# Loading q token-major behind the keys and transposing it with the DMA crossbar, in an attention and feed-forward kernel

## The chip, the cores and the metric

One Trainium2 chip, one core. The metric is the device time of one execution in microseconds (us). Profiles are single executions; the first instruction of the profile is time zero in every "at" below. The span in a profile is 1.7 to 1.8 us shorter than the time of the same execution. The granted clock is the share of TensorE's full clock that the chip allowed it, as the profile records it.

## The reference

Four batches of sparse-sorted attention feed a feed-forward layer with a squared ReLU. The feed-forward products dominate; the attention of later tiles is woven between them.

```python
B, H, S, D = 4, 8, 768, 64; n_blocks = 8          # block = 96 rows
# P: sort_net after five rounds of exp and row/column normalisation
k_sorted = einsum('bhij,bhjcd->bhicd', P, k_blocks)
v_sorted = einsum('bhij,bhjcd->bhicd', P, v_blocks)
scores   = scale * q_block @ k_sorted_block.T      # per block of 96 rows
out      = softmax(scores) @ v_sorted_block
x = out.transpose(0, 2, 1, 3).reshape(3072, 512)
g = s * relu(x @ w_in)**2 + b                      # w_in 512 x 2048
result = g @ w_out                                 # w_out 2048 x 512, float32 out
```

## The kernel before: what the change and the argument touch

A batch is two tiles of 384 tokens. QT[b] is q of a batch turned so that the head dimension lies on the partitions; the scores need it. In the kernel before, q of batch 1 comes in rows of 768 B and TensorE turns it; q of batches 2 and 3 already comes token-major (rows of 128 B) and is turned by DMA transposes (transfers that transpose on their way, through the DMA crossbar) that SP issues. Token-major means that each row of 128 B is one token of one head. Transfers issued by GpSimd are in the software queue (q0 in the profile), those of SP in the hardware queue (q1). Values of batch 1 are sorted on TensorE, stored to DRAM (`dv`) and read back in another layout (`vs`), also by SP. A GpSimd sum over w_out (`csum`) goes through one product (`bias_piece`) that stands ahead of the scores in TensorE's order.

```python
def load_q(b, part=slice(0, 128)):                 # GpSimd issues: the software queue
    if b > 1:
        qr[b] = qrp.tile([128, TQ, H, D], BF, tag="qr", name=f"qr{b}")
        for t in range(TQ):                        # six loads of 1024 rows of 128 B
            nc.gpsimd.dma_start(out=qr[b][:, t],
                in_=q[b][:, t * 128:(t + 1) * 128, :].rearrange("h p d -> p h d"))
        return
    # ... one load, rows of 768 B: "p h t d", token = 6 * p + t

# ... loads of w_out, in two halves
for f0 in range(0, NF, FW):
    # ... nc.gpsimd.dma_start(out=w, in_=moe_w_out ...)
    if f0 == 0:
        load_q(1)
load_k(*brows(1))                                  # 64 rows of 12 KB

def q_piece(b, hp0, eng):                          # 24 transposes on TensorE, one copy
    # ... nc.tensor.transpose(out=ps[...], in_=qr[b][:, 2 * (hp0 + i) + e, t, :], ...)

def q_turn(b):                                     # SP issues: the hardware queue
    QT[b] = qtp.tile([128, NHP, S], BF, tag="qt", name=f"qt{b}")
    for t in range(TQ):
        nc.sync.dma_start(out=QT[b][:, :, t * 128:(t + 1) * 128],
                          in_=qr[b][:, t].rearrange("p h d -> p (h d)"), transpose=True)

# ... the schedule around batch 1
V1(4)()                                            # the last two stores to dv
V1(5)()
q_piece(1, 0, "s")
csum = const.tile([128, d_model], FP)
# ... gate: GpSimd waits for x of tile 1
csums(0, 8)
v_read(1, nc.sync)                                 # two reads dv -> vs, 6144 rows of 128 B
ffn1(1, Queue([nothing] * 4 + [build_pd2] + [nothing] * 3, 8))
load_v(*brows(3))                                  # 64 rows of 12 KB
load_k(*brows(2))                                  # 64 rows of 12 KB
csums(8, NF)
qu = Queue([nothing, seq(lambda: q_piece(1, 2, "s"), K(1, 0, 16, "v")), nothing,
            seq(K(1, 32, 16, "s"), K(1, 64, 16, "v")), nothing,
            seq(lambda: load_q(2), bias_piece),
            V2[0], S2(2, 0), V2[1], S2(2, 2), V2[2], V2[3], P2(2, 0), V2[4], P2(2, 2), V2[5],
            # ... (S2: scores, P2: products with vs, V2: sorting of v of batches 2 and 3)
            ], 24)
ffn2(0, qu)
```

The softmax here doesn't subtract the row's maximum and nothing guards it: scores larger than these inputs give would overflow.

## Time and profile before

| kernel before | |
|---|---|
| time, median of 3 (lowest to highest) | 231.15 us (230.85 to 231.45) |
| profiled execution: time, span, mean granted clock | 232.64 us, 230.9 us, 0.978 |
| first scores of batch 1 / first products with vs | 68.49 / 76.81 us |
| packets of the software queue / hardware queue | 18800 / 27728 |

What the change takes away is in TensorE's order of instructions (start, duration, line, shapes, count), of which the kernel before has, as one of two such groups (the other is at 59.41):

```profile
45.81 0.86 PE L269 MATMUL tq<-ident,qr 128*64 128x128 bf16 x24
```

The two groups of 24 transposes are the 1.7 us that the change wants back. The page's row of the granted TensorE clock, 40 slices of some 5.8 us in tenths, is full after the start:

```profile
PEclk9985799999999999999999999999999999999999
```

### The profile page before, as it was taken

What the parts mean: (1) busy time and instruction counts of PE and PEld (TensorE: products, weight loads), DVE (VectorE), ACT (ScalarE), POOL (GpSimd) and SP (SyncE); (2) the same over time, 40 slices, a digit from 0 to 9 for tenths busy, and PEclk for the clock granted to TensorE, in tenths of its full rate; (3) what the DMA queues carried; (4) which work ended last, traced back from release to release, by engine and by line L of the source; (5) the groups of instructions that cost most, each with busy time, mean ns of one, the idle gap of its engine ahead of it and who ended that gap; (6) DMA issues with size and microseconds to landing.
All of it is one profiled execution on the core that took longest, in us unless ns stands there. A gap on an engine that the chain in (4) does not pass through costs nothing.

```text
span 230.9 us, 4813 instructions
## 1 busy us (share of the span) xinstructions
PE 221.4 (96%) x2014; PEld 135.9 (59%) x2034; DVE 116.4 (50%) x244; ACT 115.7 (50%) x165; POOL 48.2 (21%) x62
## 2 busy tenths in 40 slices
PE   8979999999999799999999999999999999999994
PEld 5869787765544456565555555665555555654442
DVE  4778666638991455244445843443443634442221
ACT  5268479675468286856630285666222236660000
POOL 7920000399992000008830000000000000000000
PEclk9985799999999999999999999999999999999999
DMA  5999999998999992745999996610115250001212
GB/s 93 144 197 214 231 186 205 232 214 193 201 78 134 266 288 81 136 116 65 127 148 146 180 184 119 90 47 0 48 45 114 94 112 2 3 0 45 82 57 91
DMA packets 46694, 28.90 MB, mean 125 GB/s; under 512 B 35920, under 2 KB 41040, under 8 KB 46160
## 3 DMA queue, kind: packets, MB, share of 16 engines
q0 software_dynamic: 18800, 15.21, 47.9%
q1 hardware_dynamic: 27728, 13.32, 25.9%
q8 instruction: 16, 0.26, 0.4%
q10 hardware_dynamic: 144, 0.07, 0.1%
q14 instruction: 6, 0.05, 0.1%
HBM read 29.63 MB, written 8.65 MB: 166 GB/s over the span
## 4 chain that ended last, share of the span: by engine, by line
PE 73%; DMA 15%; DVE 5%; ACT 3%; issue 1%; SPq 0%
PE hps L498 31%; PE ops L552 30%; DMA dv<-vn 9%; DMA vs<-dv 5%; PE pv L402 3%; PE sc L375 3%; PE tv L320 2%; PE ops L537 2%; PE tk L294 1%; ACT ks L240 1%; DVE x L407 1%; PE tq L254 1%; DMA sn<-in_sort_net_dram 1%; ACT qt L240 1%; DVE rstat L203 1%
## 5 line engine op out<-in xcount | busy, mean ns | idle before, releaser
L498 PE MATMUL hps<-xt,wi 128*128 128x384 bf16 (+1 forms) x576 | 87.0, 308 | 0.3
L552 PE MATMUL ops<-wo,gt 128*128 128x512 bf16 x348 | 82.9, 379 | 1.1 <-issue 0.2
L498 PEld LDWEIGHTS <-wi 128*128 128x128 bf16 x576 | 53.7, 98 | 30.6 <-issue 1.1
L513 ACT ACTIVATE rt<-hps 128x768 bf16<-128x768 f32 (+1 forms) x72 | 53.1, 740 | 37.1 <-PE hps L498 36.2
L514 DVE TENSOR_TENSOR gt<-rt 128x768 bf16<-128x768 bf16 (+1 forms) x72 | 42.2, 588 | 49.5 <-ACT rt L513 49.3
L552 PEld LDWEIGHTS <-gt 128*128 128x128 bf16 x368 | 34.1, 98 | 37.8 <-issue 0.6
L378 ACT ACTIVATE at<-sc 96x768 bf16<-96x768 f32 x32 | 24.4, 803 | 30.3 <-PE sc L375 30.3
L526 DVE SCALAR_TENSOR_TENSOR ot<-ops,s_bc,bias 128x512 f32<-128x512 f32 x23 | 17.2, 750 | 40.0 <-PE ops L552 39.9
L407 DVE TENSOR_TENSOR x<-pv,rec 96x512 bf16<-96x512 f32 (+1 forms) x36 | 22.6, 627 | 1.3
L240 ACT CAST ks<-tk 64x512 bf16<-64x512 f32 (+1 forms) x32 | 18.6, 581 | 4.2 <-PE tk L294 3.8
L674 POOL TENSOR_TENSOR csum<-csum,wo 128x512 f32<-128x512 f32 x14 | 17.6, 1255 | 1.0
L402 PEld LDWEIGHTS <-at 96*128 96x128 bf16 (+1 forms) x256 | 12.0, 104 | 5.5 <-DMA vs<-dv 1.9
L402 PE MATMUL pv<-vs,at 96*128 96x66 bf16 (+1 forms) x256 | 13.0, 199 | 1.5 <-DMA vs<-dv 1.4
L238 DVE CAST ks<-tk 64x512 bf16<-64x512 f32 (+1 forms) x20 | 13.1, 653 | 2.1 <-PE tk L294 1.8
L182 PE MATMUL wp<-zt 128*128 128x256 bf16 x84 | 12.8, 318 | 1.1 <-DVE warm L113 1.1
L240 ACT CAST vn<-tv 128x512 bf16<-128x512 f32 (+1 forms) x12 | 9.4, 800 | 8.0 <-PE tv L350 5.7
L406 DVE RECIPROCAL rec<-pv 96x8 f32<-96x8 f32 (+1 forms) x36 | 6.9, 191 | 10.3 <-PE pv L402 10.2
L375 PEld LDWEIGHTS <-ks 64*96 64x96 bf16 x256 | 8.3, 128 | 5.7 <-issue 4.3
L84 POOL DMA_DIRECT2D qr<-in_q_dram x12 | 10.6, 913 | 5.0 <-DMA kb<-in_k_dram 2.9
L182 PEld LDWEIGHTS <-zt 128*128 128x128 bf16 x84 | 9.1, 113 | 3.0 <-DVE warm L113 1.1
L375 PE MATMUL sc<-qt,ks 64*96 64x96 bf16 x256 | 10.7, 219 | 0.0
L240 ACT COPY qt<-tq 128x768 bf16<-128x768 bf16 (+1 forms) x6 | 5.9, 1014 | 5.0 <-PE tq L254 3.3
(72 smaller groups left out, 97.2 us busy)
## 6 DMA issues: line engine op xcount, KB each, us to landing
out_dram<-ot SPq DMA_DIRECT2D x23, 256.0 KB, 2.4
kb<-in_k_dram POOLq DMA_DIRECT2D x4, 768.0 KB, 11.2
vb<-in_v_dram POOLq DMA_DIRECT2D x4, 768.0 KB, 18.9
wi<-in_moe_w_in_dram POOLq DMA_DIRECT2D x2, 1024.0 KB, 19.6
wo<-in_moe_w_out_dram POOLq DMA_DIRECT2D x2, 1024.0 KB, 32.3
qr<-in_q_dram POOLq DMA_DIRECT2D x12, 128.0 KB, 15.2
dv<-vn SPq DMA_DIRECT2D x6, 256.0 KB, 6.9
vs<-dv POOLq DMA_DIRECT2D x4, 384.0 KB, 12.8
```

Of the source, the lines that this page charges most:

```text
L182: nc.tensor.matmul(out=wp, lhsT=zt[:, 0:128], rhs=zt, start=True, stop=True)
L240: nc.scalar.copy(out=out, in_=in_)
L375: nc.tensor.matmul(out=sc[:, e, n * BLK:(n + 1) * BLK], lhsT=ks[pr, g0 + n, :], rhs=QT[b][pr, hp, q0:q0 + BLK], start=True, stop=True)
L378: nc.scalar.activation(out=at, in_=sc[:, :, 0:TG], func=AF.Exp, scale=scale)
L402: nc.tensor.matmul(out=pv[e][0:m, (n - n0) * VW:(n - n0 + 1) * VW], lhsT=atf[:, c0:c0 + m], rhs=VS[b][:, gi, :], start=True, stop=True)
L407: nc.vector.tensor_tensor(out=x[:, n0:n0 + nn, hp * 128:(hp + 1) * 128].rearrange("p n (e d) -> p e n d", e=2), in0=pvv[:, :, :, 0:D], in1 ...
L498: nc.tensor.matmul(out=hps[:, f, 0:nt], lhsT=wi_at(hp, f0 + f), rhs=xt_at(t, hp, n0, nn), start=(hp == 0), stop=(hp == NHP - 1))
L513: nc.scalar.activation(out=rt[:, :, 0:nt], in_=hps[:, :, 0:nt], func=AF.Relu)
L514: nc.vector.tensor_tensor(out=gt[:, f0:f0 + 2, c0:c0 + nt], in0=rt[:, :, 0:nt], in1=rt[:, :, 0:nt], op=ALU.mult)
L526: nc.vector.scalar_tensor_tensor(out=ot, in0=ops, scalar=s_bc, in1=bias, op0=ALU.mult, op1=ALU.add)
L552: nc.tensor.matmul(out=ops, lhsT=gt[:, f, m * 128:(m + 1) * 128], rhs=wo_at(f), start=(f == 0), stop=(f == NF - 1))
L674: nc.gpsimd.tensor_tensor(out=csum, in0=csum, in1=wo_at(f), op=ALU.add)
```

## The change

The intent: q of batch 1 is treated as q of batches 2 and 3 already are. TensorE loses 48 transposes and ACT two copies; the load moves behind the keys of batch 1, so that w_out comes earlier; the keys of batch 2 move from the middle of GpSimd's column sums to behind them, directly ahead of q of batch 2.

```diff
--- before.py
+++ after.py
@@ -78,7 +78,7 @@
     def load_q(b, part=slice(0, 128)):
 
 
-        if b > 1:
+        if b > 0:
             qr[b] = qrp.tile([128, TQ, H, D], BF, tag="qr", name=f"qr{b}")
             for t in range(TQ):
                 nc.gpsimd.dma_start(
@@ -163,9 +163,8 @@
         nc.gpsimd.dma_start(
             out=w, in_=moe_w_out.rearrange("(f p) n -> p f n", p=128)[:, f0:f0 + FW, :])
         wos.append(w)
-        if f0 == 0:
-            load_q(1)
     load_k(*brows(1))
+    load_q(1)
 
     def wi_at(hp, f):
         return wis[f * 128 // FCH][:, hp, f * 128 % FCH:f * 128 % FCH + 128]
@@ -257,20 +256,6 @@
             evac(QT[0][:, 2 * a:2 * a + 2, half * TG:(half + 1) * TG].rearrange(
                      "q b (p t) -> q b p t", t=TQ),
                  ps[:, a, 0:2 * TG].rearrange("q (b t p) -> q b p t", b=2, t=TQ), eng)
-
-    def q_piece(b, hp0, eng):
-
-        if hp0 == 0:
-            QT[b] = qtp.tile([128, NHP, S], BF, tag="qt", name=f"qt{b}")
-        ps = psa.tile([128, 2, 1024], BF, tag="a", name="tq")
-        for i in range(2):
-            for t in range(TQ):
-                for e in range(2):
-                    nc.tensor.transpose(
-                        out=ps[e * 64:(e + 1) * 64, i, t * 128:(t + 1) * 128],
-                        in_=qr[b][:, 2 * (hp0 + i) + e, t, :], identity=ident)
-        evac(QT[b][:, hp0:hp0 + 2, :].rearrange("q a (p t) -> q a p t", t=TQ),
-             ps[:, :, 0:S].rearrange("q a (t p) -> q a p t", t=TQ), eng)
 
     def q_turn(b):
 
@@ -659,7 +644,6 @@
                    seq(V1(2), V1(3)), lambda: t_piece(1, "v")], 8), 2, 2)
     V1(4)()
     V1(5)()
-    q_piece(1, 0, "s")
 
 
     csum = const.tile([128, d_model], FP)
@@ -675,18 +659,18 @@
 
     csums(0, 8)
     v_read(1, nc.sync)
+    q_turn(1)
     ffn1(1, Queue([nothing] * 4 + [build_pd2] + [nothing] * 3, 8))
     load_v(*brows(3))
-    load_k(*brows(2))
     csums(8, NF)
 
     def K(b, c0, nc2, eng):
         return lambda: k_piece(b, c0, nc2, 1, eng)()
 
     V2 = [lambda c0=c0: v_piece2(c0, "s") for c0 in range(0, BLK, 16)]
-    qu = Queue([nothing, seq(lambda: q_piece(1, 2, "s"), K(1, 0, 16, "v")), nothing,
+    qu = Queue([nothing, K(1, 0, 16, "v"), nothing,
                 seq(K(1, 32, 16, "s"), K(1, 64, 16, "v")), nothing,
-                seq(lambda: load_q(2), bias_piece),
+                seq(lambda: load_k(*brows(2)), lambda: load_q(2), bias_piece),
                 V2[0], S2(2, 0), V2[1], S2(2, 2), V2[2], V2[3], P2(2, 0), V2[4], P2(2, 2), V2[5],
                 seq(T(2), S2(3, 0), K(2, 0, 16, "s")), P2(3, 0), nothing,
                 seq(S2(3, 2), K(2, 32, 16, "s")), nothing, P2(3, 2),
```

## The prediction

> **What bounds the kernel now.** I read the page's busy shares and its chain first, then TensorE's order of instructions around the chain's long DMA pieces, then the DMA queues in the same stretch.
>
> ```profile
> PE 221.4 (96%) x2014; PEld 135.9 (59%) x2034; DVE 116.4 (50%) x244; ACT 115.7 (50%) x165; POOL 48.2 (21%) x62
> PE 73%; DMA 15%; DVE 5%; ACT 3%; issue 1%; SPq 0%
> ```
>
> TensorE is busy 96% of a 230.9 us span, so 9.5 us of it is idle, and work taken off TensorE counts only where it isn't given back as a wait. The chain nevertheless runs 15% through DMA. Its order of time shows where:
>
> ```profile
> 42.83 11.74 DMA dv<-vn
> ...
> 54.58 9.68 DMA dv<-vn
> ...
> 64.79 11.96 DMA vs<-dv
> ```
>
> Batch 1's sorted values are stored to DRAM (dv), read back (vs), and needed by the first P.V product of batch 1. TensorE's order of instructions there:
>
> ```profile
> 65.38 1.02 PE L596 MATMUL bps<-csum,onesf 128*128 128x512 f32 x2
> ...
> 68.49 0.56 PE L375 MATMUL sc<-qt,ks 64*96 64x96 bf16 x16
> ...
> 76.81 0.71 PE L402 MATMUL pv<-vs,at 96*128 96x66 bf16 x16 [1.44 <-DMA vs<-dv]
> ```
>
> The reader is to see two points. The first scores of batch 1, which need QT of batch 1, start at 68.49. The products that need vs start at 76.81 after 1.44 us of idleness: this is all that the long DMA chain costs. Between the two lie 76.81 - 68.49 - 1.44 = 6.9 us of other TensorE work.
>
> **What the Trainium skill says.** "DMA: Bandwidth & Descriptors", section "Queues, rings and completion order": every DMA engine takes turns between the queues that have work for it, a packet at a time. The trace agrees and gives the unit. In the window 57 to 59 us, where 12 KB rows of v and k (software queue) run beside 1 KB rows of dv (hardware queue):
>
> ```profile
> q0 software_dynamic: 32, 0.39, 92.8%
> q1 hardware_dynamic: 32, 0.03, 5.9%
> ```
>
> It is one for one, 16 of each per us over 16 engines, whatever their size: a queue of small packets beside one of 12 KB packets nearly stands still. The same page, section "Issuing engines are not separate DMA queues": transfers from SP, ACT and GpSimd run on the same 16 engines, so a transpose issued by SP gets no bandwidth of its own; the dv stores (64 KB in 9.7 to 11.7 us above) agree. "TensorE: Matmul & The Clock Gate", section "Part 1: The HAM clock gate": after an idle window of some 3.4 us TensorE falls to half clock and needs as long again to recover. After the 1.44 us wait here the granted clock stays at full; no longer wait late in this trace tests it.
>
> **The change, part by part.**
>
> Removed. 48 transposes of q on TensorE, 24 before the first product of tile 1 at 45.81 (0.86 us) and 24 at 59.41 (0.80 us from its start to that of the next group): 1.7 us of TensorE, before 60.2. Two ACT copies of 1.44 us, beside TensorE's work. One 768 KB load in rows of 768 B; it sat ahead of the second half of w_out.
>
> Does the 1.7 us reach the end? The next fixed point is the bias product at 65.38, which waits for GpSimd's column sums:
>
> ```profile
> 54.58 10.61 POOL L674 TENSOR_TENSOR csum<-csum,wo 128x512 f32<-128x512 f32 x8
> 65.13 5.32 POOL L84 DMA_DIRECT2D qr<-in_q_dram x6
> ```
>
> The sums end at 65.13. The issue of batch 2's keys (0.53 us) leaves its place in front of them, so they end at about 64.6 and the bias starts at about 64.7. TensorE comes 0.7 us earlier, not 1.7; the scores could start at 67.8. Then the old 1.44 us wait for vs goes too if vs lands by 67.8 + 6.9 = 74.7. So the most the change can bring is 0.7 + 1.44 = 2.1 us.
>
> Added: six loads of 1024 packets of 128 B each, and six transposes of 512 packets of 256 B (131 KB each). Rates from windows in which one kind dominates: q's 128 B packets at 126 to 127 us, 1111 in 1 us; vs packets alone at 65.2 to 68, 2556 in 2.8 us = 913 per us; transposes at 139.5 to 142, 1820 in 2.5 us = 730 per us; transposes beside q loads at 130 to 133, 1196 against 1212 in 3 us = 400 per us each. Issuing six transposes takes SP 8.53 us, with 2.4 us (median 2.5) from issue to landing where the queue is free.
>
> Moved: the transposes stand on SP behind the two vs reads, and their data behind the 6144 packets of vs in the hardware queue. The first scores wait for three of the six (the first half of the columns, as the order of instructions shows), the later ones for the rest.
>
> When do these three land? The stores of dv should finish much sooner: in the time that they were stuck behind 12 KB packets (44 to 52 us) they now alternate with q's small packets. I estimate the last dv at 50 to 53 instead of 64.3, and the vs read starts there. But it then meets v of batch 2 and of batch 3, 64 packets of 12 KB each, 4 us apiece at 16 per us. Adding up everything ahead in the queues from 35 us, an estimate per engine from the packet times: w_out 5.3, k1 3.7, q1 6144/1111 = 5.5, v2 and v3 7.4, dv 2.2, vs 6144/913 = 6.7, sum 30.8 us, so about 65.8. Whatever the order inside, vs is drained only then: in time for its products (74.7), but the batch-2 keys are issued at 64.6 and begin at about 65.5 to 67, four 12 KB packets per engine, 3.7 us in which the transposes hardly move. They resume at 69.5 to 70.5, now against q of batch 2 (issued from 65.1 on) at 400 per us: 3 x 512/400 = 3.8 us if nothing of them went before, 2 if half did, and about 1.1 to land. The third lands at about 73.5, with 70 to 77 as a plausible spread.
>
> The sum: scores at 73.5 instead of 67.8, products of vs then at 73.5 + 6.9 = 80.4 instead of 76.81: +3.6 us. A wait of 5.7 us may also cost a microsecond of half clock, or not. After that the path is TensorE's own, shifted as a block: x of tile 2 was turned by 88.0, against its use at 92.17, so there is slack.
>
> **The rivals.**
> (a) The transposes are in time. If vs and three transposes get through before the batch-2 keys begin, nothing waits at the scores and the kernel gains the 2.1 us: 229.0. For it: my sum of 65.8 falls within 1 us of the keys' start, and in the kernel before q of batch 2, issued at 65.13, moved its first packet only at about 68.5 while vs was running; a delay like that would let 1 to 2 transposes through. Against it: the third must also be issued, and SP's next issue after vs was itself stuck for 3.92 us (68.85 to 72.77), until most of vs had gone.
> (b) A longer wait. If stragglers among the engines (the last of q2 landed at 82.67, though its bulk was through by 78) decide, the third transpose lands at 77 to 79: +7 to +9 us, plus the slower clock: 239 to 241.
> (c) vs becomes the later one. If vs were still held by the keys, its products would wait instead; but they have 6.9 us more than the scores, so (c) is hidden by (b).
> (d) GpSimd: v of batch 2 now waits for a free semaphore behind q's six loads, and could hold up the column sums; the second w_out half should land at 44 (now 48.7, less the 3.9 us of q), just when the sums begin (44.22), so at most a microsecond, itself inside the wait at the scores.
>
> **Range and chances.** The time is 231.15 + max(third transpose, 67.8) - 69.9: where 69.9 = 76.81 - 6.9. With 73.5 that is 234.7; I put 234.5, since the gain in (a) is bounded but likely enough (about 0.3) and (b) is as likely in the other direction. 8 in 10: 229 to 240. Faster by over 2% (below 226.5) needs 4.6 us, more than twice the 2.1 us there is: 0.04. Slower by over 2% (above 235.8) needs the third transpose after 74.5, or a wait that cools the clock: 0.38. Within 2%: 0.58.
>
> **What would show it.** Right: the last dv lands by 53 (now 64.26); a wait of TensorE at the scores of batch 1 put down to the transpose of qt, 3 to 8 us, in place of the 1.44 us at the products; vs lands by 71; batch-2 keys' packets between vs and the transposes. Wrong if dv still lands after 60 (then the packets' turns are not what slowed it), if the scores start by 68.5, or if vs and not qt is what TensorE waits for.

## The result, and the profile after

| | before | after |
|---|---|---|
| time, median (lowest to highest), 4 fast runs each | 231.3 us (230.85 to 231.95) | 242.79 us (241.48 to 243.87) |
| span, mean granted clock | 230.9 us, 0.978 | 242.1 us, 0.957 |
| first scores / first products with vs | 68.49 / 76.81 us | 75.80 / 88.37 us |
| packets, software / hardware queue | 18800 / 27728 | 24000 / 30992 |

The ratio is 1.0492, with a 95% interval of 1.0426 to 1.0558: slower, 242.79 us where 234.5 (229 to 240) was predicted. The spans and instants are of one profiled execution each; the changed kernel's (243.87 us) was the slowest of its four. Ratios here are the mean time of one kernel's fast runs over that of the other's fast runs of the same rounds, so not quite the ratio of the medians quoted. Executions over 1.5% slower than the fastest of the same kernel are left out of the means.

From the page after: the busy shares, the granted clock, the chain by engine, and the group of the scores (its last two fields are the idle time ahead of it and who ended it).

```profile
PE 225.1 (93%) x1986; PEld 136.4 (56%) x1986; DVE 118.1 (49%) x244; ACT 113.0 (47%) x163; POOL 52.6 (22%) x67
...
PEclk9985799999996599999999999999999999999999
...
PE 81%; DMA 7%; SPq 5%; ACT 3%; DVE 2%; issue 0%
...
L360 PE MATMUL sc<-qt,ks 64*96 64x96 bf16 x256 | 11.8, 228 | 8.8 <-DMA qt<-qr 8.8
```

TensorE has 48 instructions fewer (1986 weight loads for 2034; the matmul count of the page before, 2014, lacks 20 records) and yet no less busy time: part of it ran at a lower clock, in slices 13 and 14 (0.6 and 0.5), which are 72.6 to 84.7 us. The scores now wait 8.8 us for the transposes of q. TensorE's order of instructions in the kernel after (a wait and its releaser in brackets):

```profile
66.31 1.13 PE L581 MATMUL bps<-csum,onesf 128*128 128x512 f32 x2 [1.77 <-POOL csum L658]
...
75.80 0.31 PE L360 MATMUL sc<-qt,ks 64*96 64x96 bf16 x2 [6.21 <-DMA qt<-qr]
77.47 0.32 PE L360 MATMUL sc<-qt,ks 64*96 64x96 bf16 x2 [1.35 <-DMA qt<-qr]
79.06 0.72 PE L360 MATMUL sc<-qt,ks 64*96 64x96 bf16 x12 [1.28 <-DMA qt<-qr]
79.72 1.89 PE L537 MATMUL ops<-wo,gt 128*128 128x512 bf16 x4
...
84.90 1.04 PE L537 MATMUL ops<-wo,gt 128*128 128x512 bf16 x4
...
88.37 0.70 PE L387 MATMUL pv<-vs,at 96*128 96x66 bf16 x16
```

Three things are to be seen. First, the 1.7 us taken off TensorE came straight back as 1.77 us of waiting for the column sums; the bias product even starts 0.93 us later than before (66.31 for 65.38). Second, the scores run in three pieces, one for each transpose, with 6.21 + 1.35 + 1.28 = 8.84 us of waiting. Third, four feed-forward products that take 1.04 us at 84.90 take 1.89 us at 79.72: about half speed.

The arithmetic closes. The last piece of the scores starts 79.06 - 68.49 = 10.57 us later than before; from there to the products with vs it takes 88.37 - 79.06 = 9.31 us instead of 76.81 - 68.49 - 1.44 = 6.88, so 2.43 more; the 1.44 us wait for vs is gone. 10.57 + 2.43 - 1.44 = 11.56 us at the products with vs, and 242.1 - 230.9 = 11.2 us in the span. From there on the two kernels run alike, to within 0.4 us.

Where the transposes were, from the chain of the kernel after in order of time (start, duration, what; SPq is SP's own sequencer, L346 the reads of vs, L264 the transposes):

```profile
50.26 8.54 DMA dv<-vn
58.95 0.34 SPq L346
59.33 4.08 SPq L346
63.45 5.27 SPq L264
68.77 1.32 SPq L264
70.14 8.88 DMA qt<-qr
```

Before, the chain had dv from 54.58 to 64.3 and vs behind it. After, dv lands at 58.8 and the reads of vs are issued at 58.95 and 59.33, some 5.5 us sooner. But then SP is stuck: the first transpose takes it 5.27 us to issue. The third is issued at 70.14 and lands 8.88 us later, at 79.02. What the queues moved in those last microseconds, from the DMA view of the kernel after in the window 69 to 72 us (packets, MB, share of 16 engines):

```profile
q0 software_dynamic: 41, 0.50, 95.5%
q1 hardware_dynamic: 12, 0.00, 6.2%
```

and in the window 73 to 78 us:

```profile
q0 software_dynamic: 2181, 0.28, 92.2%
q1 hardware_dynamic: 1610, 0.39, 78.4%
```

From 69 to 72 the keys of batch 2 (rows of 12 KB) have the engines, and the hardware queue moves 12 packets in 3 us: the last 7 of vs, one of 4 B, and the first 4 of the transposes. Just before, from 67 to 69, when the keys had begun, it was the other way: 1349 hardware packets, nearly all of vs, beside 19 of the keys. From 73 to 78 the transposes share with q of batch 2: the packet records count 241 to 357 transpose packets of 256 B in each us, about 300. The three that the scores need are 1536 packets.

And GpSimd, whose sums set the start of the bias product and the issue of the keys:

```profile
45.34 0.54 POOL L100 DMA_DIRECT2D vb<-in_v_dram  x1 [6.12 <-PE tr L439]
...
66.19 0.54 POOL L97 DMA_DIRECT2D kb<-in_k_dram  x1
```

The keys are issued when the sums end, so these end at 66.2, not at 64.6 as I worked out: the sums began only behind the issue of v of batch 2, which came at 45.34. The releaser named there is only the last that the profile sees. The second half of w_out landed at 44.79, just ahead of that issue; I take the wait to be one for a DMA semaphore held by w_out or q, which no run tests.

### The profile page after: what moved, and what is told of

Read it like the earlier page. It is cut to its first block, busy times and chain, and to the rows that moved or that the text cites. A ratio compares the mean times of both kernels' runs of the same rounds, so it can differ in the third digit from the quotient of the medians.

```text
span 242.1 us, 4753 instructions
## 1 busy us (share of the span) xinstructions
PE 225.1 (93%) x1986; PEld 136.4 (56%) x1986; DVE 118.1 (49%) x244; ACT 113.0 (47%) x163; POOL 52.6 (22%) x67
## 3 DMA queue, kind: packets, MB, share of 16 engines
q1 hardware_dynamic: 30992, 14.11, 29.3%
## 4 chain that ended last, share of the span: by engine, by line
PE 81%; DMA 7%; SPq 5%; ACT 3%; DVE 2%; issue 0%
PE ops L537 31%; PE hps L483 31%; PE wp L181 5%; DMA qt<-qr 4%; DMA dv<-vn 4%; PE pv L387 4%; PE sc L360 3%; SPq L264 3%; SPq L346 2%; PE tv L305 2%; PE ops L522 1%; PE tk L279 1%; ACT ks L239 1%; PE tv L335 1%; ACT rt L498 1%; PE tq L253 1%
## 5 line engine op out<-in xcount | busy, mean ns | idle before, releaser
L537 PE MATMUL ops<-wo,gt 128*128 128x512 bf16 x368 | 87.6, 385 | 0.0
L499 DVE TENSOR_TENSOR gt<-rt 128x768 bf16<-128x768 bf16 (+1 forms) x72 | 43.6, 610 | 47.6 <-ACT rt L498 47.3
L84 POOL DMA_DIRECT2D qr<-in_q_dram x18 | 15.9, 905 | 25.7 <-DMA wi<-in_moe_w_in_dram 10.1
L360 PE MATMUL sc<-qt,ks 64*96 64x96 bf16 x256 | 11.8, 228 | 8.8 <-DMA qt<-qr 8.8
L360 PEld LDWEIGHTS <-ks 64*96 64x96 bf16 x256 | 9.1, 135 | 15.3 <-issue 14.3
L181 PE MATMUL wp<-zt 128*128 128x256 bf16 x84 | 13.5, 329 | 1.1 <-DVE warm L113 1.1
```

Of the source, the lines that this page charges most:

```text
L181: nc.tensor.matmul(out=wp, lhsT=zt[:, 0:128], rhs=zt, start=True, stop=True)
L360: nc.tensor.matmul(out=sc[:, e, n * BLK:(n + 1) * BLK], lhsT=ks[pr, g0 + n, :], rhs=QT[b][pr, hp, q0:q0 + BLK], start=True, stop=True)
L499: nc.vector.tensor_tensor(out=gt[:, f0:f0 + 2, c0:c0 + nt], in0=rt[:, :, 0:nt], in1=rt[:, :, 0:nt], op=ALU.mult)
L537: nc.tensor.matmul(out=ops, lhsT=gt[:, f, m * 128:(m + 1) * 128], rhs=wo_at(f), start=(f == 0), stop=(f == NF - 1))
```

## The experiments

Eleven kernels, in three calls; kernels of one call ran on one chip beside the same runs of the kernel before (median of 7: 231.11, 231.47 and 231.36 us). All give the reference's result. The theory at the start: the crossbar transposes stand in the hardware queue behind vs and are then pushed aside by the keys and by q of batch 2, and TensorE's clock falls in the wait. The changed kernel itself was not run again; comparisons with it are across chips. The rivals: the keys' new place is to blame; the small packets of the new load are to blame; the size of the packets (one turn each) decides, so smaller rows would free the queue; the clock is most of it.

For all of them the same few instants tell most; from TensorE's order of instructions of each:

| run | last piece of scores | first products with vs | between | span | span less products |
|---|---|---|---|---|---|
| before | 68.49 | 76.81 (1.44 of it waiting) | 8.32 | 230.9 | 154.1 |
| keys_moved_only | 68.80 | 75.51 | 6.71 | 229.6 | 154.1 |
| load_moved_only | 69.36 | 76.07 | 6.71 | 230.2 | 154.1 |
| before_small_rows | 70.23 | 76.94 | 6.71 | 231.6 | 154.7 |
| three_first | 71.06 | 77.77 | 6.71 | 232.6 | 154.8 |
| loads_held | 73.52 | 81.77 | 8.25 | 236.7 | 154.9 |
| q_held | 75.45 | 84.62 | 9.17 | 238.4 | 153.8 |
| after | 79.06 | 88.37 | 9.31 | 242.1 | 153.7 |
| q_turned_only | 80.70 | 88.67 | 7.97 | 242.4 | 153.7 |
| kept_warm | 79.90 | 88.18 | 8.28 | 241.9 | 153.7 |
| kept_warm_longer | 82.13 | 88.83 | 6.70 | 242.6 | 153.8 |

The two runs whose profile fell in the slow state, turn_first and after_small_rows, are left out. The last column is nearly constant: what the change does is done by the first product with vs. The column "between" is 6.7 us at full clock and up to 9.3 at a lower one.

### keys_moved_only

The kernel before with the keys of batch 2 in their new place, nothing else:

```diff
     load_v(*brows(3))
-    load_k(*brows(2))
...
-                seq(lambda: load_q(2), bias_piece),
+                seq(lambda: load_k(*brows(2)), lambda: load_q(2), bias_piece),
```

> The kernel before with only the last part of the change: keys of batch 2 issued behind the column sums, just ahead of q of batch 2. Theory (turns: the hardware queue gets one small packet for one 12 KB packet, so it stands still beside v and k): dv lands at about 60.5 instead of 64.3 because only v of batch 3 is left beside it, but the keys now stand in the way of vs from 65.5 to 70, so vs lands at 75 to 76.5, much as before: 230 to 231.5 us, ratio 0.995 to 1.0. Rival (moving the keys is itself what costs in the changed kernel): over 235 us.

231.36 us (230.94 to 231.75), ratio 0.9994 [0.9945, 1.0043]: the same, as expected. The last dv landed at 60.65 instead of 64.26 and there was no wait at the products with vs, yet the time stayed. This run's profiled execution was at its median (231.34 us, span 229.6), that of the kernel before was 1.5 us above its own: that suggests that the 1.44 us wait was not there to be won in a usual execution.

### q_turned_only

The changed kernel with the keys back at their old place:

```diff
     load_v(*brows(3))
+    load_k(*brows(2))
     csums(8, NF)
...
-                seq(lambda: load_k(*brows(2)), lambda: load_q(2), bias_piece),
+                seq(lambda: load_q(2), bias_piece),
```

> The changed kernel with the keys of batch 2 back at their old place, in front of the second half of the column sums. Theory (turns): the keys' 12 KB packets now hold up vs from 61 to 65 instead of the transposes from 67 to 72; vs then runs beside q of batch 2, and the third transpose lands at 77 to 80, much as in the changed kernel: 240 to 244 us. Rival (the keys' new place is the main cost): third transpose by 74, 235 to 237 us.

244.31 us (243.93 to 244.99), ratio 1.0557 [1.0512, 1.0601]. TensorE's order of instructions of this run:

```profile
77.86 0.31 PE L360 MATMUL sc<-qt,ks 64*96 64x96 bf16 x2 [8.66 <-DMA qt<-qr]
79.83 0.32 PE L360 MATMUL sc<-qt,ks 64*96 64x96 bf16 x2 [1.66 <-DMA qt<-qr]
80.70 0.71 PE L360 MATMUL sc<-qt,ks 64*96 64x96 bf16 x12 [0.56 <-DMA qt<-qr]
```

The wait is longer, 10.9 us: the keys, issued at 54.73 instead of 66.19, now fall into vs, whose second read landed at 74.92 (72.63 after). The time and the landing (80.65) came just beyond what I expected (240 to 244 us, 77 to 80). The keys' new place is not the cause: with the old one the loss is no smaller. By the medians the new place even helps by 1.5 us, but the intervals of the two ratios overlap.

### load_moved_only

The changed kernel with its load and its order of issues, but the turning done by TensorE (48 transposes and two ACT copies, in the first products of w_out), and no crossbar for batch 1:

```diff
-    q_turn(1)
...
+    def q_piece(b, hp0, eng):      # as in the kernel before, from the token-major qr
+        ...
-    qu = Queue([nothing, K(1, 0, 16, "v"), nothing,
+    qu = Queue([lambda: q_piece(1, 0, "s"), seq(lambda: q_piece(1, 2, "s"), K(1, 0, 16, "v")), nothing,
```

> The changed kernel with q of batch 1 loaded as in the change (six token-major pieces behind batch 1's keys) and the keys of batch 2 moved, but with q turned by TensorE again (48 transposes at the start of the first products with w_out, ACT copies). If it is the crossbar's transposes that cost, as my explanation has it, the scores start at about 69.4 (behind the column sums, whose wait hides the 1.7 us of TensorE), vs lands by 72.6, the first products of vs start by 77, and the time is 230 to 232 us. If the load's new place and its small packets cost by themselves, it is over 235 us.

231.89 us (231.7 to 232.65) in three fast runs, a fourth of 235.75 us was slow; ratio 1.0038 [1.0008, 1.0068]: the same within 2%, as expected (230 to 232). Its order of instructions has no wait at either place:

```profile
69.36 0.56 PE L373 MATMUL sc<-qt,ks 64*96 64x96 bf16 x16
...
76.07 0.70 PE L400 MATMUL pv<-vs,at 96*128 96x66 bf16 x16
```

So neither the 6144 packets of 128 B of q nor the order of the issues costs much: 0.5 us by the medians of fast runs, 0.9 by the ratio. This run differs from the changed kernel only in who turns q (and where TensorE does it), and is 10.9 us faster (231.89 for 242.79; 0.5 us over its own runs of before, against 11.5). The loss is that of the crossbar transposes, standing where they stand in the hardware queue.

### loads_held and q_held

In loads_held, GpSimd first copies one element that the third transpose writes, and so issues the keys and q of batch 2 only when it has landed. In q_held only q of batch 2 is held, the keys go as in the change.

```diff
+    gate1 = sk.tile([1, 1], BF)
+    def hold():
+        nc.gpsimd.tensor_copy(out=gate1, in_=QT[1][0:1, NHP - 1, S // 2 - 1:S // 2])
...
-                seq(lambda: load_k(*brows(2)), lambda: load_q(2), bias_piece),
+                seq(hold, lambda: load_k(*brows(2)), lambda: load_q(2), bias_piece),   # loads_held
+                seq(lambda: load_k(*brows(2)), hold, lambda: load_q(2), bias_piece),   # q_held
```

> The changed kernel, with the keys and q of batch 2 held back on GpSimd by a one-element copy that reads the third transposed piece of q of batch 1. Theory (the transposes wait for the turns of the two loads): vs still drains at about 68.5, then three transposes need 2 to 3 us, third lands at 72 to 72.5, first scores at 72.3 instead of 79.06, 233 to 235 us. Rival (the transposes are late because they stand behind 6144 packets of vs and are slow to be issued): they land at 76 or later, 238 us or more.

> The changed kernel with only q of batch 2 held back until the third transpose of batch 1; the keys of batch 2 are issued at once, as in the change. loads_held (both held) took the third landing from 79.0 to 73.5. If each of the two loads costs about half of the 5.5 us: third landing at 75.5 to 76.5, 239.5 to 241.5 us. If the keys' packets alone are the barrier and q costs nothing: 78 to 79 and 242 to 243.5; if q alone: 73.5 and 238.

loads_held: 238.32 us (237.49 to 238.45), ratio 1.0287 [1.0243, 1.033]. q_held: 240.46 us (239.7 to 240.92), ratio 1.0402 [1.0367, 1.0437]. TensorE's order of instructions of loads_held:

```profile
69.85 0.24 PE L360 MATMUL sc<-qt,ks 64*96 64x96 bf16 x2 [0.33 <-DMA qt<-qr]
70.85 0.24 PE L360 MATMUL sc<-qt,ks 64*96 64x96 bf16 x2 [0.76 <-DMA qt<-qr]
73.52 0.47 PE L360 MATMUL sc<-qt,ks 64*96 64x96 bf16 x12 [2.42 <-DMA qt<-qr]
...
75.92 1.91 PE L537 MATMUL ops<-wo,gt 128*128 128x512 bf16 x4
...
98.28 3.90 PE L483 MATMUL hps<-xt,wi 128*128 128x384 bf16 x23 [1.16 <-DMA xt<-x]
```

and of q_held:

```profile
74.92 0.31 PE L360 MATMUL sc<-qt,ks 64*96 64x96 bf16 x2 [5.60 <-DMA qt<-qr]
75.45 1.17 PE L360 MATMUL sc<-qt,ks 64*96 64x96 bf16 x14 [0.22 <-DMA qt<-qr]
```

The third transpose landed at 73.47 in loads_held, 75.86 in q_held and 79.02 in the change. So, each read from one profile, the keys cost 2.4 us and q of batch 2, on top of them, 3.2 us; q_held came as expected for two loads of about equal cost (75.5 to 76.5, 239.5 to 241.5 us). What is left at 73.5, with nothing in the other queue, comes from the hardware queue itself: the second vs read landed at 69.26, SP issued the three transposes at 63.96, 68.24 and 69.54. That I had predicted this same 73.5 with both loads in play is a coincidence. I had expected more of loads_held, 233 to 235 us with a landing at 72 to 72.5; its time is the rival's (238 or more), its landing isn't (76 or later). Besides the microsecond of the later landing, two reasons for the miss can be read off: the clock fell here too (four products in 1.91 us at 75.92; 8.25 us instead of 6.7 between scores and products: 1.5 us), and the loads that were held now collide with the transpose of x of tile 2, issued at 88.29 and landed at 98.14, for which TensorE waits 1.16 us.

### kept_warm and kept_warm_longer

The changed kernel with dummy products (56, then 94) ahead of the first scores, so that TensorE is not idle in the wait.

```diff
-                V2[0], S2(2, 0), V2[1], ...
+                V2[0], seq(lambda: warm_up(94, psa), S2(2, 0)), V2[1], ...
```

> The changed kernel with 56 idle products (zeros, result unused) of TensorE put just ahead of the first scores of batch 1, to fill most of the wait. If the slow clock after the wait costs what the trace suggests (79.06 to 88.37 us against 6.9 us before: 2.4 us), the scores still start at 79.1, the granted clock stays at full, and the time falls by 2 to 2.6 us to about 240.3. If the clock is not it (the products after the wait are slow for another reason), the time stays at 242 to 243.

> As kept_warm, with 94 idle products instead of 56: the first run left 4 us of wait after them, and the products behind still ran at half clock, so it did not test the clock. 94 of 0.11 us reach to 79.5. If the slow clock costs 1.5 to 2.4 us, the products after the scores now take 1.03 us per four instead of 1.9, and the time is 240 to 241.5; if not, 242 to 244.

kept_warm: 243.64 us (242.3 to 244.21) in three fast runs, a fourth of 246.37 us was slow; ratio 1.0513 [1.0452, 1.0575]. Its 56 products ended at 75.4, 4.5 us before the last piece of the scores; three waits were left (1.10, 1.78, 1.09 us) and the next four products still took 1.89 us. It did not do what it was made for, its time is above both that I had named (240.3; 242 to 243), and it says nothing of the clock's share.

kept_warm_longer: 241.76 us (240.86 to 244.3), ratio 1.0467 [1.0401, 1.0532]. The 94 products reached over the whole wait. The view by stretches (stretch, its length, busy time of PE, PEld, DVE, ACT and POOL, granted clock, DMA share, GB/s), of the changed kernel:

```profile
74.00:78.00 4.00, 0.63 (x4) 0.39 (x5) 0.00 (x0) 0.00 (x0) 0.00 (x0) 0.59 1.75 142
78.00:82.00 4.00, 2.94 (x18) 1.45 (x18) 0.00 (x0) 1.50 (x2) 0.00 (x0) 0.50 1.99 149
```

and of kept_warm_longer:

```profile
74.00:78.00 4.00, 4.00 (x40) 3.57 (x38) 0.00 (x0) 0.00 (x0) 0.00 (x0) 1.00 1.91 118
78.00:82.00 4.00, 4.00 (x39) 3.52 (x36) 0.00 (x0) 0.00 (x0) 0.00 (x0) 1.00 1.84 137
```

The granted clock stays at 1.00 instead of 0.59 and 0.50 (PEclk is the field after the engines' busy times), and from scores to products takes 6.70 us instead of 9.31. So the fallen clock costs 2.6 us between scores and products. The time does not confirm it: it is 1 us lower by the medians, with overlapping intervals of the two ratios, because the dummies overran the third transpose by 1.1 us and that transpose itself came later in the profiled run (81.03 for 79.02), which was the slowest of its four and had a slow stretch of its own before (the bias product took 2.07 us instead of 1.13, after 2.56 us of waiting).

### before_small_rows and after_small_rows

The loads of keys of batches 1 and 2 and of values of batches 2 and 3, each in two interleaved halves with rows of 2 KB instead of 12 KB, in the kernel before and in the changed one. If each packet takes a turn whatever its size, the hardware queue gets six times as much beside them.

```diff
+            if rows.start in (64, 128):
+                for l in range(2):
+                    nc.gpsimd.dma_start(
+                        out=kb[prow].rearrange("p (h l m) d -> p l h (m d)", l=2, m=16)[:, l],
+                        in_=kraw[rows].rearrange("r (h l m) d -> r l h (m d)", l=2, m=16)[:, l])
+                continue
         # ... and the same in load_v for rows.start > 64
```

> The kernel before with the same 2 KB packets. Theory: dv lands at 56 to 58 instead of 64.3, vs by 71 instead of 76.8, so the wait of 1.44 us at the first products of batch 1 is gone: 229 to 230.5 us, ratio 0.992 to 0.997. Rival: dv still lands after 63 and nothing changes.

> The changed kernel with keys of batch 1, values of batches 2 and 3 and keys of batch 2 each loaded as two interleaved halves, so that a packet is 2 KB instead of 12 KB (same bytes, one more issue each). Theory (one packet each in turn): the hardware queue gets some 90 packets per us beside them instead of 16, the last dv lands at 52 to 54 instead of 58.8, vs drains by 65, the third transpose lands at 73 to 75; the additional waits for free semaphores make the column sums 2 us later. 236 to 239 us. Rival (12 KB packets aren't what holds the hardware queue): dv at 58 to 59, vs as before, 242 to 245 us.

before_small_rows: 232.57 us (232.07 to 233.33), ratio 1.0054 [1.002, 1.0089]. The last dv landed at 56.53 instead of 64.26, which agrees with the idea. But the time did not fall to the 229 to 230.5 us that I expected: the column sums ended later (bias product at 67.01 after 0.92 us of waiting), which I put down to the additional issues on GpSimd.

after_small_rows: 238.35 to 245.91 us in four runs, of which only one (238.35) counts as fast, so there is no ratio. Its profile (242.90 us) is of a slow run, so what follows is a hint only. In the window 71 to 75 us, when the keys' rows of 2 KB go and the third transpose waits, the DMA view has:

```profile
q0 software_dynamic: 258, 0.50, 95.7%
q1 hardware_dynamic: 54, 0.01, 2.4%
```

The software queue moves its smaller packets and the hardware queue still all but stands, 54 packets in 4 us; the third transpose landed at 79.12, where I expected 73 to 75. As far as this profile goes, the rival "packet size" fails for this stretch: the hardware queue is pushed aside by a load of 2 KB rows as well.

### turn_first

The changed kernel with the transposes issued ahead of the vs reads.

```diff
-    v_read(1, nc.sync)
     q_turn(1)
+    v_read(1, nc.sync)
```

> The changed kernel with the six transposes issued on SP ahead of the two reads of vs instead of behind them. Theory: the transposes then drain as soon as the 12 KB packets of the values end (61 us), the third lands at 63 to 66 and the first scores don't wait (they start at 69.4, behind the column sums); but vs now starts at 65 and meets the keys from 67 on, lands at 80 to 83, and the first products of batch 1 wait for vs instead: 236 to 239 us. Rival (transposes are slow wherever they stand): third after 72 and 242 us or more.

243.97 us (242.36 to 245.11) in four fast runs, with two slow ones of 251.47 and 262.62 us; ratio 1.0544 [1.0482, 1.0607]: no better than the change; the rival's number ("242 or more") held, the theory's did not. The profiled execution was slow (251.47 us), so the following is a hint only. The transposes, the last dv stores and v of batch 3 then went at the same time and all crawled: v of batch 3 took 17.7 us from issue to landing (7.4 in the change), the third transpose landed at 76.21 although issued at 55.66, and the longest wait moved to the products with vs, 8.01 us ahead of 93.54. So putting all six in front seems only to move the crowd to an earlier place.

### three_first

The last form, from what was learned: only the three transposes that the first scores need go ahead of the vs reads, the other three behind; v of batch 3 is issued after four more column sums, so that it doesn't meet them; the keys and q of batch 2 are held until vs has landed.

```diff
-    v_read(1, nc.sync)
-    q_turn(1)
+    q_turn(1, 0, 3)
+    v_read(1, nc.sync)
+    q_turn(1, 3, 6)
...
-    load_v(*brows(3))
-    csums(8, NF)
+    csums(8, 12)
+    load_v(*brows(3))
+    csums(12, NF)
...
+    # hold() as above, on VS[1][:, 63, D - 1:D]; then load_k(2), load_q(2)
```

> An attempt to keep the crossbar and lose nothing: the three transposes that the first scores need are issued ahead of the vs reads, the other three behind them; the values of batch 3 are loaded four column sums later (about 61 instead of 55), and keys and q of batch 2 wait until vs has landed. Theory (every transfer that is in flight with the transposes takes its time from them): the three land at 60 to 64 with only the tail of the values of batch 2 beside them, vs at 72 to 75, neither the scores nor the products wait; 230 to 232.5 us. Rival (transposes hold up the whole hardware queue wherever they are put, as in turn_first, where v of batch 3 took 17.7 us): vs after 78 and 235 us or more.

234.07 us (233.28 to 236.74), ratio 1.0145 [1.0081, 1.0208]: unclear, between "same" and "slower" by the 2% rule, and above the 230 to 232.5 us that I expected. The three transposes landed at 59.74, 59.93 and 60.13, eleven microseconds before the scores, which start at 71.06 without a wait; vs landed at 72.40, and its products did not wait either. What is left, from TensorE's order of instructions:

```profile
69.67 0.59 PE L336 MATMUL tv<-vb,pd 128*128 128x512 bf16 x2 [1.75 <-DMA vb<-in_v_dram]
...
94.10 4.06 PE L484 MATMUL hps<-xt,wi 128*128 128x384 bf16 x24 [0.98 <-DMA xt<-x]
```

Two waits of 2.7 us together, for v of batch 3, which was delayed on purpose, and for x of tile 2, against the delayed loads. With these the crossbar is kept and most of the loss is gone, but nothing tried here beats the kernel before.

## Why the prediction was wrong, step by step

- **What the change can win** (at most 0.7 + 1.44 us): an upper bound that held, but too kind. The 0.7 us supposed sums at 64.6; they ended at 66.2, since the issue of v of batch 2 waited until 45.34 and the sums began 1.6 us later than before (46.01 for 44.43). That was rival (d), for which I had allowed at most a microsecond, hidden inside the wait at the scores. It was not quite hidden: the keys' issue moved with it, from 64.6 to 66.19. The 1.44 us may not exist in a usual execution (keys_moved_only).
- **The mechanism** (scores wait for the third transpose, in place of the products' wait for vs; vs lands in time; the keys stand between vs and the transposes): right. TensorE waited 8.8 us, put down to qt, and never for vs. load_moved_only shows that the turning by the crossbar is nearly the whole loss. Of the signs that I had named, the place of the keys and the wait at the scores came (8.84 us, just over my 3 to 8); dv by 53 and vs by 71 did not (58.8 and 72.63).
- **The failed step: "the third lands at about 73.5".** It landed at 79.02. Term by term, from the packet records: the transposes resume at 72.2, as the keys' last packets go, where I had 69.5 to 70.5. For the keys were issued 1.6 us later than I had reckoned, and their 64 packets ran from 67.8 to 73.6, 5.8 us, where I had 3.7. The 1536th packet of the transposes starts at 77.6, after 5.4 us at some 284 per us, where I had 2 to 3.8 us at 400; and it is another 1.4 us to the landing, where I had 1.1. 72.2 + 5.4 + 1.4 = 79.0. The runs say the same another way: 73.5 is what remains when neither load is there (loads_held); keys add 2.4 us, q of batch 2 adds 3.2 on top.
- **"One for one, whatever their size"**: right for the pair from which I read it, wrong as a rule. Beside q's starting loads dv got far less: in the window 47 to 50 us of the changed kernel, 252 hardware packets against 2704 of the software queue. So the last dv landed at 58.8, not 50 to 53, when v of batch 2 was in its way again. And beside the keys the hardware queue got 1349 for 19 from 67 to 69 us and 12 for 41 from 69 to 72. The test that I had named ("wrong if dv lands after 60") missed it by being too loose.
- **The queue's sum** (vs drained at 65.8): nearly all of its packets had gone by 68.4. From 61 to 68, alone for most of that time, vs ran at 480 to 1244 packets per us, 818 on average, where I had 913: 6144 packets take 7.5 us instead of 6.7. The rest comes with the late dv, behind which vs is issued only at 58.95.
- **The clock** ("a microsecond of half clock, or not"): 2.4 us by the two intervals, 2.6 by kept_warm_longer. I had counted one wait of 5.7 us; the scores came in three pieces with little work between them, and the slow stretch went on to about 84.
- **The sum**: with the third transpose at 79.02 the formula gives 231.15 + 79.0 - 69.9 = 240.3, and with 2.4 us of clock 242.7; measured 242.79. The formula stood; its argument was 5.5 us off and the clock 1.4. Rival (b), 77 to 79 and 239 to 241, was nearly the case, though not by stragglers alone: the 1536 packets as a whole were late.

What stays open: why the hardware queue is pushed aside as far as it is beside a load that has begun (12 for 41; 54 for 258 with 2 KB rows, in a slow run), and why not in the two microseconds before (1349 for 19). The packet's size is not the whole answer, as far as these windows go; the runs do not show the cause.

## What to carry to other kernels

A DMA transpose moves work off TensorE, but puts it into a queue; when it lands was set here by what stood ahead of it in its own queue (vs) and by what the other queue started meanwhile (the two loads moved the landing from 73.5 to 79.0). Before trading 1.7 us of TensorE for it, list both, and ask when the first consumer needs it. A share of bandwidth read from one pair of transfers holds for that pair; read it again for each pair that will meet. A wait that came in pieces with little work between cost its length and then 1.5 us (loads_held) to 2.6 us of lower clock.

## What the Trainium skill lacked or had wrong

- "DMA: Bandwidth & Descriptors", "Queues, rings and completion order": it says that an engine drains a whole packet, typically some 9 to 17 descriptors, from one queue before it switches. I took the profile's packets for these. In the changed kernel's window 47 to 50 us there are 2704 / 252 = 10.7 software packets of mostly 128 B for each hardware packet, 10.6 (1146 / 108) from 44 to 46: this would fit the page if what the profile counts is a descriptor, and dv's were turns of one. No run shows whether that is the reason. Nor does the page let one tell beforehand why rows of 12 KB went 32 : 32 with dv (kernel before, 57 to 59 us), but 19 : 1349 and then 41 : 12 with what stood in the hardware queue of the changed kernel (67 to 69 and 69 to 72 us).
- The same page, "Rules for kernel authors": "A transpose next to ordinary DMAs needs nothing." The sentence is about silent corruption, and there these runs agree, all results were right. What the page lacks is the time: the third transpose took 8.9 us from issue to landing next to ordinary loads, 3.9 us without them (loads_held), 2.4 us on a free queue (kernel before).
- The same page, "Issuing engines are not separate DMA queues": the sequencer's time to initiate a DMA is called usually small relative to the DMA. Here SP was held 5.27 us by one transpose of 131 KB while vs drained, and 8.56 us in three_first, both times with vs still unfinished in the same queue.
- "TensorE: Matmul & The Clock Gate", "Part 1: The HAM clock gate": agrees in kind (granted clock 0.50 and back to 1.00). It gives no lengths for waits that are broken by short work: 0.33 + 0.76 + 2.42 us were followed by a clock of 0.62 and then 0.52 in loads_held (74 to 78 us), which cost 1.5 us; 8.84 us in three pieces cost 2.4.
